# New priorities for the planner of an attention and two-layer expert kernel, and one scaling moved from POOL to ScalarE

## The chip, the cores and the metric

The kernel runs on one core of a Trainium2 chip. Times are device microseconds of one execution. A run is repeated and its median is given; a profile is one further execution, which has its own time and its own span (first to last instruction). The engines are TensorE (PE: matmuls, and PEld for its weight loads), VectorE (DVE), ScalarE (ACT), GpSimd (POOL) and SyncE (SP), which issues most transfers.

## The reference

Three stages follow each other on 4 batches x 576 positions x 512 features.

```python
# 1 attention: q, k, v of (4, 8, 576, 64)
q_d, k_d, v_d = means over groups of 4 positions        # 144 of them
out_d = softmax(q_d k_d^T / 8) v_d, each row repeated 4 times
scores = q k^T / 8 where |i - j| < 4, else -1e9
x = out_d + softmax(scores) v                            # then (2304, 512)
# 2 experts: one of 8 for each token
e = argmax(x w_gate);  g = softmax(x w_gate)[e] * sigmoid(x w_output_gate)[e]
x = g * (relu(x w1[e]) w2[e])                            # 512 -> 1024 -> 512
# 3 a dense layer
h = relu(x w_in);  out = (h * h) w_out                   # 512 -> 2048 -> 512
```

## The kernel before, in words

**Attention** goes by batch. For each batch `b` the keys and queries are loaded in two halves (`load`), folded to 144 positions (`fold`: keys on VectorE, queries on POOL) and the keys are copied into block form on ScalarE (`kb`). The coarse attention has five units `u` per batch: scores (`ds_s`, TensorE), maximum (`ds_m`, VectorE), its scaling (`ds_b`, ScalarE), exponential (`ds_e`, ScalarE, tile `pd`), a small constant added (`ds_a`, ScalarE), reciprocal (`ds_r`, VectorE), the product (`ds_n`, POOL), transposes (`ds_t`, TensorE), copies out (`ds_c`, ScalarE). `ds_pv` and `ds_po` finish it with the folded values (`vd_p`, `vd_c`). The local attention has three units `t3` per batch, in the same manner: `lc_s` (64 small matmuls, L621), `lc_m`, `lc_d` (VectorE), `lc_e` (ScalarE, tile `e`), `lc_v` (the sum, VectorE, L639), `lc_a` (ScalarE), `lc_r` (VectorE), `lc_n` (POOL), `lc_t` (VectorE), then `pv_mm` (128 small matmuls, L672) with the value tiles of `load_vw`. `pv_ad` adds both results into `xT` (VectorE).

**Routing** of a batch: logits (`rt_l`, `rt_le`, `rt_sel`, `rt_lc`), one-hot choice (`rt_g1`), positions (`rt_pp`, `rt_pos`, `rt_base`), the gate's factor (`rt_g2`, `rt_ex`, `rt_ez`, `rt_sm` at L754, `rt_g3`), lists of tokens (`rt_ids` with the marks of L823, `rt_tk` on TensorE at L836, `rt_to`). The tokens are transposed (`rt_bt`), scaled by the factor on their way out of PSUM (`rt_xs`) and stored to DRAM (`rt_st`). In the last batch copying out (`rt_xe`) and scaling (`rt_xs`) are two steps, and the five tiles are scaled by different engines.

**Experts.** The expert with most tokens after three batches goes first, with 256 rows (index -1). Then all eight go by rank, with fixed capacities of 368 to 208 rows. For each expert: rows are gathered by a list (`gather`, POOL; the list comes from `fa_i` or `fr_i`), transposed (`turn`), and written as a high and a low part (`x_hi` on ScalarE, L1150; `x_lo` on VectorE, L1155); the weights are loaded in four steps each (`load1`, `load2`) and split in the same way (`w1_hi`, `w1_lo` at L1172, `w2_hi`, `w2_lo` at L1179). Each product is three matmuls, high by high, high by low and low by high: `mm_h` (L1189) and `mm_y` (L1213). `y_out` and `y_st` store the result. The dense layer's weights are converted from 64-bit floats beside the experts (`cl`, `cm`, `cb`, `ch`, `cx`), and the **dense layer** runs in six windows of 384 rows (`mm1` at L1363, `mm2` at L1387).

**The order** of all this is made by class `Plan` before the program is built. Every operation is entered with its engine, a duration in ns, a number `prio`, what it depends on, and the ring of buffers it takes. `order` then goes forward in a model of time: among the operations that are ready it takes the one that can start first, and where several can start at the same moment, the one with the lowest `prio`:

```python
c = (t, d["prio"], o)
if best is None or c < best:
    best = c
```

The instructions of each engine, transfers of SyncE included, are issued in the order of these planned starts, and each engine works its own list in order. The planned times themselves are not in the program: on the chip, an instruction starts when what it waits for is there and the one before it on its engine has been issued. `SHIFT` holds a number for a kind of operation, which is added to `prio`. One unit of `prio` is a third of a batch in attention and one step of an expert's loop of eight in the experts.

Of the kernel before, what the change touches and what calls it, by code (L numbers as in the profile page):

```python
# [12 lines left out]
ALU = mybir.AluOpType  # L13
# [33 lines left out]
def bcast(ap, shape):  # L47
    return ap.to_broadcast(shape)


SHIFT = {"cho": -1.28, "cli": -7.75, "cmi": 5.29, "cmo": -13.66, "cz": -0.76, "ds_c": 3.91, "ds_m": -18.08, "h_lo": 1.7,
         "kb": 0.72, "lc_e": 1.51, "lc_m": -6.57, "lc_v": 28.85, "mm2": 5.8, "mm_h": -2.09, "mm_y": -0.22, "pv_ad": -13.75,
         "rt_l": -0.15, "rt_ot": 2.89, "rt_pos": 5.92, "rt_sm": 5.36, "rt_xs": 13.38, "turn": 0.29, "vd_c": 18.07,
         "w2_lo": -7.1}


class Plan:
# [9 lines left out]
    def op(self, kind, key, eng, dur, prio, fn, deps=(), lat=0, dma=0, take=None, pair=()):  # L67


        o = (kind,) + key  # L70
        prio += SHIFT.get(kind, 0)
        if isinstance(dur, list):
            run = []

            def step(last):
                if not run:
                    run.append(fn(*key))
                next(run[0], None)
                for _ in run[0] if last else ():
                    pass  # L80

            for i, d in enumerate(dur):
                last = i == len(dur) - 1
                oi = o if last else o + ("step", i)
                self.ops[oi] = dict(eng=eng, dur=d, prio=prio, fn=lambda last=last: step(last), lat=lat, dma=dma, pair=i in pair,
                                    deps=list(deps) if i == 0 else [o + ("step", i - 1)], take=take if i == 0 else None)
            self.first[o] = o + ("step", 0) if len(dur) > 1 else o
            return
        self.ops[o] = dict(eng=eng, dur=dur, prio=prio, fn=lambda: fn(*key), deps=list(deps), lat=lat, dma=dma, take=take, pair=0 in pair)
# [69 lines left out]
class Kern:  # L159
# [194 lines left out]
    def plan_b(self, b):  # L354
        op = self.plan.op
        s = 3.0 * b
# [16 lines left out]
        for u in range(NPR + 1):  # L373
            tau = s - 1.1 + 0.42 * u
            w = 1.0 if u < NPR else 0.6
            pd = "pd" if u < NPR else "pl"
            k = (b, u)
            op("ds_s", k, "PE", 540, tau, self.ds_s, [("fold", b, nm, t) for nm in "kq" for t in range(2) if u // 2 >= t] + [("ds_s", b - 1, 4)] + [("ds_pv", b - 1, 1)] * (u > 1), take="pds")
            op("ds_m", k, "DVE", 365 * w, tau + 0.06, self.ds_m, [("ds_s",) + k])
            op("ds_b", k, "ACT", 100, tau + 0.1, self.ds_b, [("ds_m",) + k])  # L380
            op("ds_e", k, "ACT", 620 if u < NPR else 310, tau + 0.16, self.ds_e, [("ds_b",) + k] + [("ds_e", b - 1, i) for i in range(5)], take=pd)
            self.plan.give("pds", ("ds_s",) + k, ("ds_e",) + k)
            op("ds_a", k, "ACT", 100, tau + 0.2, self.ds_a, [("ds_e",) + k])
            op("ds_r", k, "DVE", 65, tau + 0.22, self.ds_r, [("ds_a",) + k])
            op("ds_n", k, "POOL", 575, tau + 0.3, self.ds_n, [("ds_r",) + k], pair=(0,))
            op("ds_t", k, "PE", 490 if u < NPR else 260, tau + 0.44, self.ds_t, [("ds_n",) + k, ("ds_pv", b - 1, 1)], take="ptr")
            self.plan.give(pd, ("ds_e",) + k, ("ds_t",) + k)
            op("ds_c", k + (0,), "ACT", 270, tau + 0.5, self.ds_ca, [("ds_t",) + k])
            op("ds_c", k + (1,), "ACT", 270, tau + 0.5, self.ds_cv, [("ds_t",) + k])
            self.plan.give("ptr", ("ds_t",) + k, ("ds_c",) + k + (0,), ("ds_c",) + k + (1,))  # L390
# [5 lines left out]
        for t3 in range(3):  # L396
# [5 lines left out]
            self.plan.give("psc", ("lc_s",) + i, ("lc_d",) + i)  # L402
            op("lc_e", i, "ACT", 530, k + 0.47, self.lc_e, [("lc_d",) + i])
            op("lc_v", i, "DVE", 590, k + 0.54, self.lc_v, [("lc_e",) + i])
            op("lc_a", i, "ACT", 110, k + 0.54, self.lc_a, [("lc_v",) + i])
            op("lc_r", i, "DVE", 160, k + 0.54, self.lc_r, [("lc_a",) + i])
            op("lc_n", i, "POOL", 970, k - 0.38, self.lc_n, [("lc_r",) + i], pair=(0,))
            op("lc_t", i, "DVE", 610, k + 0.78, self.lc_t, [("lc_n",) + i], take="pT")
# [37 lines left out]
        for t in range(TPB):  # L446
# [4 lines left out]
            if last:  # L451
                op("rt_xe", (b, t), "ACT", 480, tau + 0.38 + 0.08 * t, self.rt_xe, [("rt_bt", b, t)], take=ring)
                self.plan.give("ptr", ("rt_bt", b, t), ("rt_xe", b, t))
                op("rt_xs", (b, t), ("ACT", "ACT", "POOL", "DVE", "ACT")[t], (600, 600, 1230, 400, 600)[t], tau + 0.19, self.rt_xs, [("rt_xe", b, t), ("rt_g3", b)])
            else:
                op("rt_xs", (b, t), "ACT", 580, tau + 0.4 + 0.08 * t, self.rt_xs, [("rt_bt", b, t)], take=ring)
                self.plan.give("ptr", ("rt_bt", b, t), ("rt_xs", b, t))
# [319 lines left out]
    def rt_xs(self, b, t):  # L777
# [4 lines left out]
            nc.scalar.activation(xo[:n], self.T.pop(("bt", b, t))[:n].rearrange("p c d -> p (c d)"), AF.Copy, scale=s[:n, t:t + 1])  # L782
            return
        xo = self.T["xo", b, t]
        if t == 2:
            nc.gpsimd.tensor_tensor(xo[:n], xo[:n], bcast(s[:n, t:t + 1], [n, DM]), op=ALU.mult)
        elif t != 3:
            nc.scalar.activation(xo[:n], xo[:n], AF.Copy, scale=s[:n, t:t + 1])
        else:
            nc.vector.tensor_scalar(xo[:n], xo[:n], s[:n, t:t + 1], None, op0=ALU.mult)  # L790
# [845 lines left out]
```

## Time and profile before

| | |
|---|---|
| median of 3 runs | 820.26 us (lowest 819.17) |
| profiled execution | 819.88 us, span 818.1 us |
| mean granted clock of TensorE | 0.966 |
| TensorE busy | 763.2 us, 93% |
| VectorE busy | 462.5 us, 57% |
| ScalarE busy | 373.2 us, 46% |
| POOL busy | 117.0 us, 14% |

Busy shares are averages over the whole span. Attention and routing take about the first fifth of it, the experts end near 400 us, and the dense layer takes the rest. The granted clock is the share of full speed that TensorE got, 1.00 for 2.4 GHz and 0.50 for 1.2 GHz; over a stretch it is a mean of the two.

### The profile page before, as it was taken

To read this page: it belongs to the slowest core of one execution; us is meant where nothing else is said; L and a number is where in the kernel's file an instruction comes from. 1 tells how busy PE (TensorE), PEld (TensorE's weight loads), DVE (VectorE), ACT (ScalarE), POOL (GpSimd) and SP (SyncE) were. 2 spreads that over 40 slices of the span, in tenths; PEclk is the share of its full clock that TensorE was granted. 3 is DMA by queue.
4 is the path that set the end of the run, shared out by engine and by line. 5 is a ranking of instruction groups with operands and counts; after the bars stand their busy time and mean duration, and the time that the engine had idled before them with its cause. 6 is when DMAs were issued, how large, how long until landed. Compare 5 with 4: busy or idle time off the path is not lost.

```text
span 818.1 us, 16969 instructions
## 1 busy us (share of the span) xinstructions
PE 763.2 (93%) x6764; PEld 688.6 (84%) x6764; DVE 462.5 (57%) x1022; ACT 373.2 (46%) x801; POOL 117.0 (14%) x150
## 2 busy tenths in 40 slices
PE   3788888698999999999999999999999999999994
PEld 2556566698999999999999989988999999999993
DVE  7647464666877788888687774275223223223221
ACT  9864574544565566667454532222223223222221
POOL 7634220120110110000123301010001001001001
PEclk9968998699999999999999999999999999999997
DMA  9534554667676688787343402011002001001001
GB/s 358 205 94 132 170 174 147 204 204 230 217 226 204 219 251 258 236 251 248 128 142 126 141 1 78 1 40 39 1 1 77 1 1 40 1 0 39 1 1 41
DMA packets 65092, 100.77 MB, mean 123 GB/s; under 512 B 4956, under 2 KB 43356, under 8 KB 65008
## 3 DMA queue, kind: packets, MB, share of 16 engines
q1 hardware_dynamic: 61888, 89.68, 33.9%
q0 software_dynamic: 3120, 9.95, 3.5%
q8 instruction: 55, 0.90, 0.5%
q14 instruction: 29, 0.24, 0.1%
HBM read 80.23 MB, written 19.38 MB: 122 GB/s over the span
## 4 chain that ended last, share of the span: by engine, by line
PE 80%; issue 9%; DVE 3%; ACT 1%; DMA 1%; POOL 0%; another core or an unknown queue 0%; POOLq 0%; DVEq 0%; ACTq 0%
PE hp L1363 21%; PE op L1387 20%; PE hp L1189 14%; PE yp L1213 13%; PE po L672 2%; PE sc L621 1%; PE tp L770 1%; PE dsp L600 1%; PE xp L1144 1%; DMA r<-in_moe_w_dram 1%; PE tp L690 1%; PE tp L568 1%; PE tp L701 1%; PE dsp L522 1%; PE tp L569 1%
## 5 line engine op out<-in xcount | busy, mean ns | idle before, releaser
L1363 PE MATMUL hp<-yh,winh 128*128 128x384 f32 x384 | 129.5, 337 | 0.0
L1363 PE MATMUL hp<-yh,winl 128*128 128x384 f32 x384 | 129.4, 337 | 0.0
L1363 PE MATMUL hp<-yl,winh 128*128 128x384 f32 x384 | 129.3, 337 | 0.0
L1371 DVE SCALAR_TENSOR_TENSOR r<-hp,r 128x384 f32<-128x384 f32 x96 | 53.4, 557 | 120.5 <-ACT r L1368 120.1
L1368 ACT ACTIVATE r<-hp 128x384 f32<-128x384 f32 x96 | 47.2, 492 | 153.5 <-PE hp L1363 143.9
L1387 PE MATMUL op<-woh,hl 128*128 128x512 f32 x288 | 113.8, 395 | 0.2 <-DVE hl L1379 0.2
L1387 PE MATMUL op<-woh,hh 128*128 128x512 f32 x288 | 113.8, 395 | 0.0
L1387 PE MATMUL op<-wol,hh 128*128 128x512 f32 x288 | 113.0, 392 | 0.0
L1379 DVE TENSOR_TENSOR hl<-r,hh 128x384 fp32r<-128x384 f32 x96 | 56.7, 592 | 93.0 <-ACT hh L1375 93.0
L1375 ACT ACTIVATE hh<-r 128x384 fp32r<-128x384 f32 x96 | 50.3, 524 | 112.9 <-PE op L1387 112.2
L1189 PE MATMUL hp<-xh,w1h 128*128 128x256 f32 (+7 forms) x288 | 87.2, 303 | 7.0 <-DVE k L826 5.6
L1189 PE MATMUL hp<-xl,w1h 128*128 128x256 f32 (+7 forms) x288 | 86.5, 300 | 1.5 <-DVE xl L1155 1.5
L1189 PE MATMUL hp<-xh,w1l 128*128 128x256 f32 (+7 forms) x288 | 86.4, 300 | 0.0
L1213 PE MATMUL yp<-hh,w2h 128*128 128x368 f32 (+7 forms) x256 | 76.1, 297 | 0.0
L1213 PE MATMUL yp<-hl,w2h 128*128 128x368 f32 (+7 forms) x256 | 75.8, 296 | 0.0
L1213 PE MATMUL yp<-hh,w2l 128*128 128x368 f32 (+7 forms) x256 | 75.8, 296 | 0.0
L1363 PEld LDWEIGHTS hp<-yh,winh 128*128 128x128 f32 x384 | 72.1, 188 | 3.7
L1363 PEld LDWEIGHTS hp<-yl,winh 128*128 128x128 f32 x384 | 72.1, 188 | 3.6
L1363 PEld LDWEIGHTS hp<-yh,winl 128*128 128x128 f32 x384 | 72.1, 188 | 0.0
L1387 PEld LDWEIGHTS op<-woh,hl 128*128 128x128 f32 x288 | 54.0, 188 | 13.4 <-DVE hl L1379 0.6
L1397 POOL DMA_INDIRECT out_dram<-oo,tidc x18 | 17.9, 993 | 316.2 <-DVE oo L1392 191.0
L1189 PEld LDWEIGHTS hp<-xh,w1h 128*128 128x128 f32 x288 | 55.9, 194 | 7.7 <-issue 5.9
(276 smaller groups left out, 1459.7 us busy)
## 6 DMA issues: line engine op xcount, KB each, us to landing
r<-in_moe_w_dram SPq DMA_DIRECT2D x72, 512.0 KB
raw<-in_moe_w_in_dram SPq DMA_DIRECT2D x16, 512.0 KB
raw<-in_moe_w_out_dram SPq DMA_DIRECT2D x16, 512.0 KB
vw<-in_v_dram SPq DMA_DIRECT2D x12, 512.0 KB
kT<-in_k_dram SPq DMA_DIRECT2D x8, 576.0 KB
qT<-in_q_dram SPq DMA_DIRECT2D x8, 576.0 KB
yT_dram<-zero SPq DMA_DIRECT2D x8, 576.0 KB
yr<-yT_dram SPq DMA_DIRECT2D x6, 768.0 KB
```

The lines of the kernel that those rows point to most:

```text
L522: nc.tensor.matmul(out=sv[:, 0, :], lhsT=qdbd[:, u, 0:P], rhs=kds[:, u], start=True, stop=True)
L568: nc.tensor.transpose(out=tq[:, P * a:P * a + P], in_=pf[:, a, 0:P], identity=ident)
L672: nc.tensor.matmul(out=po[HD * a:HD * a + HD, i, c0:c0 + QB], lhsT=vw[r, g2, 2 * pr + a, :], rhs=pT[r, g2 * 8 + pr * 2 + a, 0:QB], start=T ...
L1189: nc.tensor.matmul(out=ps[:, :cap], lhsT=a[:, k, :], rhs=b[:, k, :cap], start=(n == 0), stop=(n == 11))
L1213: nc.tensor.matmul(out=Y[r][c][:, :cap], lhsT=a[:, P * c:P * c + P], rhs=b[:, :cap], start=(f == 0 and n == 0), stop=(f == 7 and n == 2))
L1363: nc.tensor.matmul(out=ps[:, :WN], lhsT=a[:, k, :], rhs=b[:, k, :], start=(n == 0), stop=(n == 11))
L1368: nc.scalar.activation(r, PS[w, f][:, :WN], AF.Relu)
L1371: nc.vector.scalar_tensor_tensor(SQ[w, f], PS[w, f][:, :WN], 0.0, SQ[w, f], op0=ALU.max, op1=ALU.mult)
L1375: nc.scalar.activation(SQ[w, f, 1][0], SQ[w, f], AF.Copy)
L1379: nc.vector.tensor_tensor(sl, SQ[w, f], sh.bitcast(F32), op=ALU.subtract)
L1387: nc.tensor.matmul(out=O[w][t], lhsT=a[:, P * t:P * t + P], rhs=b, start=(f == 0 and n == 0), stop=(f == 15 and n == 2))
L1397: ins = nc.gpsimd.indirect_dma_start(out=self.out, out_offset=bass.IndirectOffsetOnAxis(ap=self.tidc[:, 3 * w + t:3 * w + t + 1], axis=0), ...
```

## The change

`SHIFT` is replaced by a table of other numbers, and it can now also hold a number for one batch, one expert or one setup step of a kind: `"lc_s:3"` is the local scores of batch 3, `"turn:0"` the transposes of the first ranked expert, `"w1_lo:-1"` the low first-layer weights of the early expert, `"cz:sel"` the setup step `sel`. Such a number is added to that of its kind. Two durations that the planner uses are raised, those of `ds_a` and `lc_a`. In the last batch the scaling of tile 2 moves from POOL to ScalarE, in the plan and in the program. Kinds that are no longer in the table (`cmi`, `lc_v` without a batch, `mm_y`, `rt_sm`, `w2_lo` and others) go back to no shift. Nothing else differs: apart from that scaling every instruction is the same.

```diff
--- before.py
+++ after.py
@@ -48,10 +48,14 @@
     return ap.to_broadcast(shape)
 
 
-SHIFT = {"cho": -1.28, "cli": -7.75, "cmi": 5.29, "cmo": -13.66, "cz": -0.76, "ds_c": 3.91, "ds_m": -18.08, "h_lo": 1.7,
-         "kb": 0.72, "lc_e": 1.51, "lc_m": -6.57, "lc_v": 28.85, "mm2": 5.8, "mm_h": -2.09, "mm_y": -0.22, "pv_ad": -13.75,
-         "rt_l": -0.15, "rt_ot": 2.89, "rt_pos": 5.92, "rt_sm": 5.36, "rt_xs": 13.38, "turn": 0.29, "vd_c": 18.07,
-         "w2_lo": -7.1}
+SHIFT = {"cho": -7.05, "cli": -6.63, "cmo": -9.74, "cz:pn2": 0.51, "cz:qd1": -1.14, "cz:sel": 17.29, "cz:tri": 3.98,
+         "ds_a": 2.2, "ds_c": 3.14, "ds_c:0": 0.13, "ds_c:1": -17.69, "ds_e": 2.74, "ds_m": -16.61, "ds_pv:3": 2.23,
+         "ds_r": -2.37, "ds_t:0": -1.38, "ds_t:1": 2.98, "ds_t:3": -0.27, "fr_i:0": 6.28, "h_lo:-1": 1.97, "kb:1": 6.47,
+         "kb:2": -12.83, "lc_e": 4.13, "lc_m": -1.86, "lc_n": -0.86, "lc_n:1": -2.11, "lc_r": -1.14, "lc_r:1": 0.6,
+         "lc_s:2": 4.65, "lc_s:3": 8.3, "lc_v:0": 7.03, "lc_v:1": 6.09, "load_vw:0": -8.32, "mm2": 5.54, "mm_h": -1.92,
+         "pv_ad": -20.14, "pv_mm:1": 3.06, "pv_mm:2": 0.13, "rt_base:0": 4.94, "rt_bt:0": 1.18, "rt_g2": -11.79,
+         "rt_l:2": -0.17, "rt_ot": -4.8, "rt_ot:1": 1.18, "rt_pos": 5.97, "rt_sel:0": 2.2, "rt_tk:1": 3.47, "rt_xs": 12.75,
+         "turn": 0.53, "turn:0": -4.59, "vd_c": 9.22, "vd_p:3": 3.55, "w1_lo:-1": 1.19, "y_out": -4.5}
 
 
 class Plan:
@@ -68,7 +72,7 @@
 
 
         o = (kind,) + key
-        prio += SHIFT.get(kind, 0)
+        prio += SHIFT.get(kind, 0) + SHIFT.get(f"{kind}:{key[0]}" if key else "", 0)
         if isinstance(dur, list):
             run = []
 
@@ -380,7 +384,7 @@
             op("ds_b", k, "ACT", 100, tau + 0.1, self.ds_b, [("ds_m",) + k])
             op("ds_e", k, "ACT", 620 if u < NPR else 310, tau + 0.16, self.ds_e, [("ds_b",) + k] + [("ds_e", b - 1, i) for i in range(5)], take=pd)
             self.plan.give("pds", ("ds_s",) + k, ("ds_e",) + k)
-            op("ds_a", k, "ACT", 100, tau + 0.2, self.ds_a, [("ds_e",) + k])
+            op("ds_a", k, "ACT", 185, tau + 0.2, self.ds_a, [("ds_e",) + k])
             op("ds_r", k, "DVE", 65, tau + 0.22, self.ds_r, [("ds_a",) + k])
             op("ds_n", k, "POOL", 575, tau + 0.3, self.ds_n, [("ds_r",) + k], pair=(0,))
             op("ds_t", k, "PE", 490 if u < NPR else 260, tau + 0.44, self.ds_t, [("ds_n",) + k, ("ds_pv", b - 1, 1)], take="ptr")
@@ -402,7 +406,7 @@
             self.plan.give("psc", ("lc_s",) + i, ("lc_d",) + i)
             op("lc_e", i, "ACT", 530, k + 0.47, self.lc_e, [("lc_d",) + i])
             op("lc_v", i, "DVE", 590, k + 0.54, self.lc_v, [("lc_e",) + i])
-            op("lc_a", i, "ACT", 110, k + 0.54, self.lc_a, [("lc_v",) + i])
+            op("lc_a", i, "ACT", 195, k + 0.54, self.lc_a, [("lc_v",) + i])
             op("lc_r", i, "DVE", 160, k + 0.54, self.lc_r, [("lc_a",) + i])
             op("lc_n", i, "POOL", 970, k - 0.38, self.lc_n, [("lc_r",) + i], pair=(0,))
             op("lc_t", i, "DVE", 610, k + 0.78, self.lc_t, [("lc_n",) + i], take="pT")
@@ -451,7 +455,7 @@
             if last:
                 op("rt_xe", (b, t), "ACT", 480, tau + 0.38 + 0.08 * t, self.rt_xe, [("rt_bt", b, t)], take=ring)
                 self.plan.give("ptr", ("rt_bt", b, t), ("rt_xe", b, t))
-                op("rt_xs", (b, t), ("ACT", "ACT", "POOL", "DVE", "ACT")[t], (600, 600, 1230, 400, 600)[t], tau + 0.19, self.rt_xs, [("rt_xe", b, t), ("rt_g3", b)])
+                op("rt_xs", (b, t), ("ACT", "ACT", "ACT", "DVE", "ACT")[t], (600, 600, 600, 400, 600)[t], tau + 0.19, self.rt_xs, [("rt_xe", b, t), ("rt_g3", b)])
             else:
                 op("rt_xs", (b, t), "ACT", 580, tau + 0.4 + 0.08 * t, self.rt_xs, [("rt_bt", b, t)], take=ring)
                 self.plan.give("ptr", ("rt_bt", b, t), ("rt_xs", b, t))
@@ -782,9 +786,7 @@
             nc.scalar.activation(xo[:n], self.T.pop(("bt", b, t))[:n].rearrange("p c d -> p (c d)"), AF.Copy, scale=s[:n, t:t + 1])
             return
         xo = self.T["xo", b, t]
-        if t == 2:
-            nc.gpsimd.tensor_tensor(xo[:n], xo[:n], bcast(s[:n, t:t + 1], [n, DM]), op=ALU.mult)
-        elif t != 3:
+        if t != 3:
             nc.scalar.activation(xo[:n], xo[:n], AF.Copy, scale=s[:n, t:t + 1])
         else:
             nc.vector.tensor_scalar(xo[:n], xo[:n], s[:n, t:t + 1], None, op0=ALU.mult)
```

## Rows read from the trace of the kernel before

**Rows 1.** Stretches: length; busy PE, PEld, DVE, ACT, POOL; clock, DMA share, GB/s

```profile
0.00:20.00 20.00, 6.69 (x110) 4.72 (x114) 14.80 (x48) 19.00 (x20) 14.07 (x40) 1.00 0.93 357
20.00:135.00 115.00, 96.14 (x2603) 69.12 (x2592) 69.94 (x201) 71.32 (x220) 37.46 (x53) 0.90 0.44 144
135.00:165.00 30.00, 21.86 (x244) 18.03 (x242) 18.45 (x61) 14.61 (x29) 3.15 (x3) 0.66 0.68 221
165.00:200.00 35.00, 31.68 (x226) 30.80 (x225) 19.75 (x42) 15.48 (x31) 7.46 (x7) 0.95 0.73 229
200.00:807.00 607.00, 606.47 (x3602) 565.90 (x3600) 339.11 (x673) 252.22 (x502) 52.06 (x46) 1.00 0.32 101
```

**Rows 2.** TensorE in order of time, two local score runs: start, us, operation

```profile
23.59 1.10 PE L621 MATMUL sc<-kbd,qT 128*32 128x64 f32 x64
...
60.37 1.94 PE L621 MATMUL sc<-kbd,qT 128*32 128x64 f32 x64
```

**Rows 3.** Waits of TensorE, 20 to 135 us: total, times, longest

```profile
PE po L672 <- issue: 6.3, 6, 2.2
PE dsp L526 <- issue: 3.8, 1, 3.8
PE dsp L526 <- ACT pd L544: 1.6, 2, 0.9
PE dsp L522 <- ACT pd L544: 1.5, 1, 1.5
```

**Rows 4.** POOL in order of time, the scaling that moves

```profile
153.44 1.04 POOL L786 TENSOR_TENSOR xo<-xo,s 128x512 f32<-128x512 f32 x1 [7.15 <-DVE pi L818]
```

**Rows 5.** VectorE in order of time, 151 to 157 us

```profile
151.18 0.68 DVE L1179 TENSOR_TENSOR w2l<-r,w2h 128x512 fp32r<-128x512 f32 x1
...
152.15 0.19 DVE L754 TENSOR_REDUCE sm<-ex 128x5 f32<-128x40 f32 x1
...
153.44 1.32 DVE L790 TENSOR_SCALAR xo<-xo,s 128x512 f32<-128x512 f32 x1
154.68 0.81 DVE L823 TENSOR_TENSOR bm<-iob,pi 128x640 bf16<-128x640 f32 x1
155.42 0.68 DVE L1155 TENSOR_TENSOR xl<-hp,xh 128x512 fp32r<-128x512 f32 x1
...
156.73 0.68 DVE L1155 TENSOR_TENSOR xl<-hp,xh 128x512 fp32r<-128x512 f32 x1
```

**Rows 6.** Instructions of line L1311: ns min/median/max, first and last start

```profile
L1311 DVE TENSOR_SCALAR f<-f x32: 411/422/1066, 198.7 to 468.9; 128x512 f32<-128x512 f32 x32
```

**Rows 7.** ScalarE in order of time, 150 to 155 us

```profile
150.66 0.58 ACT L1150 ACTIVATE xh<-hp 128x512 fp32r<-128x512 f32 x1
153.38 1.33 ACT L788 ACTIVATE xo<-xo,s 128x512 f32<-128x512 f32 x2 [2.15 <-DVE pi L818]
154.62 0.57 ACT L1150 ACTIVATE xh<-hp 128x512 fp32r<-128x512 f32 x1
```

**Rows 8.** Waits of TensorE, 135 to 200 us

```profile
PE hp L1189 <- DVE k L826: 5.6, 1, 5.6
PE hp L1189 <- DVE xl L1155: 1.5, 2, 0.8
PE hp L1189 <- ACT xh L1150: 1.5, 1, 1.5
```

**Rows 9.** TensorE in order of time, two instructions between 170 and 187 us

```profile
170.56 0.35 PE L836 MATMUL tp<-dg,bm 128*128 128x80 bf16 x5
...
186.69 0.44 PE L1189 MATMUL hp<-xh,w1h 128*128 128x368 f32 x1 [1.46 <-ACT xh L1150]
```

**Rows 10.** DMA issues, the value tiles: count, size

```profile
vw<-in_v_dram SPq DMA_DIRECT2D x12, 512.0 KB
```

**Rows 11.** Waits of TensorE, 0 to 20 us

```profile
PE dsp L522 <- ACT pd L544: 4.8, 1, 4.8
```

**Rows 12.** Waits of VectorE, 20 to 160 us, the local softmax's sum

```profile
DVE lsm L639 <- ACT e L635: 3.7, 4, 1.1
```

## The prediction

> **What bounds the kernel now.** I began with the busy times by stretch, then read the waits of the stretches with holes, then the instruction order in the two worst holes. From 200 us on TensorE is busy for 606.47 of 607 us at a granted clock of 1.00 [rows 1]. That part has a fixed length, and the end of the kernel is the moment at which it begins plus that length. VectorE and ScalarE have 339 and 252 us of work in these 607, so they cover their own reordering there. Everything that this change can give or take lies before 200 us.
>
> There TensorE is idle for 13.3 us in the first 20, for 18.9 us from 20 to 135 (attention), for 8.1 us from 135 to 165 (the last batch's routing and the early expert) and for 3.3 us from 165 to 200 (the start of the first ranked expert): 43.6 us [rows 1]. It is also slow there. The same 64 score matmuls take 1.10 us at 23.6 us and 1.94 us at 60.4 us [rows 2]: the two levels of its clock, 2.4 and 1.2 GHz. Busy time times the missing clock gives what that costs: 0.10 of 96.1, 0.34 of 21.9 and 0.05 of 31.7 are 9.6, 7.4 and 1.6, together 18.6 us [rows 1]. So 62 us stand against the change as a ceiling that no order reaches, because the first loads and the first folds are part of it.
>
> Not all of the idle time is a matter of order. Of the 18.9 us in attention, 6.3 and 3.8 are "issue" [rows 3]: TensorE waited for nothing that the profile shows, mostly between the small matmuls of one instruction run. A priority cannot remove these 10.1 us. The other 8.8 us are waits for work of other engines, the largest named ones for ScalarE's exponentials (`pd`), 1.6 and 1.5.
>
> **Part 1, the scaling moved from POOL to ScalarE.** Removed: one POOL multiply of 1.04 us [rows 4]. It starts at 153.44 us, the same moment as VectorE's scaling of another tile, which takes 1.32 us [rows 5]. The nearest row without POOL beside it is L1311, also a tensor-by-scalar operation on 128x512 from SBUF to SBUF, with a median of 0.42 us [rows 6]. The scaling stands in front of the marks (L823) and the two low parts of the early expert's rows (L1155), and TensorE starts its long run only behind the second of these [rows 5]. Between a gain of 0 (the scalar is a tile here, a constant there) and 0.9 I take 0.9, the value of the nearest row. The Trainium skill ("Advanced Engine Details and Errata", VectorE Performance Modes) says that VectorE's second SBUF port is shared with GpSimd and that the two block each other; by that rule it is 0.9 us, without it 0. Added: one ScalarE scaling, 0.67 us by the pair that takes 1.33 [rows 7]. ScalarE had idled 2.15 us just before that pair, and behind it stands the second high part (154.62 us). If the third scaling goes ahead of it, that ends at 155.9 instead of 155.2; the low part that needs it would, with VectorE 0.9 us earlier, start at 155.8. So the cover is just used up, and the cost is 0 (0.7 if VectorE gains more than that). POOL's queue issues nothing else until the gathers of the first ranked expert, so POOL's relief is worth nothing. **-0.9**
>
> **Part 2, the two model durations.** 100 to 185 ns and 110 to 195 ns issue no instruction. They only move the planner's ScalarE clock, 32 times 85 ns over the four batches. 0 by themselves; they act through the order, counted below.
>
> **Part 3, the order from 135 to 165 us.** TensorE waits 5.6 us for VectorE in front of the early expert [rows 8]. The first high part of its rows is ready at 151.24 us (150.66 + 0.58 [rows 7]), but its low part runs at 155.42 [rows 5]. In between VectorE does low parts of second-layer weights (L1179, 0.6 us from start to start; two of them stand directly ahead), the ordering of experts, and late (152.15 us) the softmax sum of the routing, which is what the scalings wait for. The change takes the low second-layer weights' head start away (-7.1 to 0), moves the softmax sum forward (+5.36 to 0) and the gate product too (to -11.79). The two weight parts behind the rows: 1.2 us. Of the remaining 5.6 - 0.9 - 1.2 = 3.5 us I take a quarter, 0.9: several things must move together (the scale, then ScalarE's scalings, then the second high part). Ends: 0 and the whole 4.7. What is late next is the second high part on ScalarE. **-2.1**
>
> **Part 4, the first ranked expert.** TensorE waits 1.5 us for its high part and 1.5 us for low parts [rows 8]; at 186.69 us one matmul has started and the run waits [rows 9]. Its transposes get a much lower number (-4.06 on balance), but its list of rows gets a higher one (+6.28), and the placing matmul (L836, 170.56 us [rows 9]) behind which that list stands stays where it was. If two list operations fall behind two low weight parts, the gathers and all behind them come 2 x 0.69 = 1.4 us later. Ends: -3.0 and +1.4; I take the middle. **-0.8**
>
> **Part 5, attention, 20 to 135 us.** Some forty numbers change here: the local softmax's sum loses its 28.85 in the last two batches, the additions into `xT` go further ahead, the third batch's key copies go first, the second's later. These are the same instructions on the same engines, and ScalarE and VectorE are busy 71 and 70 of 115 us [rows 1], so neither is the bound; the waits come from order and latency. Ends: all 8.8 us of waits gone, or 4 us more; a quarter gone is my estimate, as in part 3, where I could name the pieces and the named ones came to about a third. **-2.2**
>
> **Part 6, the start.** The first batch's value tiles are asked for before the second batch's keys and queries. Each is 512 KB [rows 10], 1.5 us at the 357 GB/s of that stretch, where the DMA share is 0.93 [rows 1]. Three of them delay the second batch's data by 4.4 us. ScalarE is busy for 19.0 of the first 20 us, and its 4.8 us of delay to TensorE [rows 11] is work, not order. Ends: -4.8 and +4.4; 0 is taken, since ScalarE has the same work to get through in either order.
>
> **Part 7, the clock.** Of the 18.6 us lost, 7.4 hang on the hole that part 3 narrows and 9.6 on attention's. I let a quarter come back, as much as of the waits. **-4.6** (ends 0 and 18.6.) The Trainium skill ("TensorE: Matmul & The Clock Gate", Part 1) puts the warm-up at under 1% of a typical kernel's span and advises against fitting a model to it, since where the change of level falls differs from run to run. By it at most 8.2 us could be had, and none counted on; in this trace the loss is 2.3% of the span.
>
> **The dense part** (second-layer numbers, output copies, conversion of weights): 0. Its cover is the idle 268 us of VectorE and 355 of ScalarE; where it fails, TensorE's idle time is paid in full.
>
> **Sum:** 0.9 + 2.1 + 0.8 + 2.2 + 4.6 = 10.6 us. The profiled execution took 819.88 us (span 818.1), 0.4 under the median of 820.26. 819.9 - 10.6 = 809.3, and 809.7 against the median: 810.
>
> **Rivals.**
> *Larger gain, 0.25.* The order fits the chip better than a quarter: part 1, all of part 3 (4.7), half of the rest (1.5, 4.4 and 9.3): 20.8 us, 799. For it: the holes are latencies, not work. Against: 10.1 us of issue time and the busy start stay.
> *No change, 0.13.* Each wait removed returns as another, because the planner picks among ready operations by earliest start and the number only breaks ties; many new numbers then give nearly the old order. For it: waits in attention are short and spread over many causes. 819.5.
> *The clock does not follow, 0.10.* Waits shrink as forecast, but the slow stretches stay where they are: 6.0 us, 814. This is the skill's advice above, carried out.
> *Slower, 0.10.* VectorE blocks on the local softmax's sum. Its number falls while that of the exponential before it rises (1.51 to 4.13). VectorE takes its instructions in order, so where ScalarE is later than planned, the maxima, additions and transposes behind the sum wait, and then TensorE. Before, 4 of 12 sums waited, 3.7 us in all, 1.1 at most [rows 12]. It decides when the other 8 wait too: 8 x 1.1 = 8.8 us, of which some two thirds reach TensorE: 826; if the clock falls in those holes, about as much again.
>
> **How the numbers follow.** Forecast 0.42. The range 797 to 823 leaves out the best part of the larger gain (0.07) and most of the slower case (0.08). 2% is 16.4 us, about what a measurement of this kernel can tell from no change. Below 803.9: the larger gain almost whole and the lower edge of the forecast, 0.27. Above 836.7: half of the slower case, 0.05. The rest, 0.68, lies within.
>
> **What would show it.** VectorE's scaling at about 0.42 us; TensorE's 5.6 us wait at 3 or less; the dense part starting some 10 us earlier and as long as before; a clock above 0.90 and 0.66 in the two stretches; the issue time near 10 us. I am wrong if the dense part shows holes, if the clock alone moves the sum, or if VectorE's waits for the exponential grow.

## The result, and the profile after

The kernel after took a median of 809.54 us (805.0 to 811.17, 12 runs) against 818.35 us for the kernel before on the same chip (12 runs): a ratio of 0.9897, 95% interval 0.9871 to 0.9924, so 8.8 us or 1.0% less by the medians. One of the 12 runs of before took 2564.57 us; the ratio leaves it out, and without it the medians are 8.0 us apart. Its profiled execution took 811.17 us with a span of 809.3 us, 8.8 us less than the 818.1 us of before.

To see where they come from I mark four events that every kernel has: the selection matmul of the last batch (**sel**, L701 before, L705 after), the second matmul of the early expert's run (**run**), the last second-layer group of the experts (**last y**), and the end. From the last y to the end both kernels take 413.4 us.

| us | to sel | sel to run | run to last y | span |
|---|---|---|---|---|
| before | 143.3 | 14.1 | 247.3 | 818.1 |
| after | 145.8 | 8.0 | 242.2 | 809.3 |
| difference | +2.5 | -6.1 | -5.1 | -8.8 |

The work on either side of sel is not quite the same. Of the last batch's 20 transposes (`rt_bt`), 12 stand behind sel in the order of before and 4 in that of after; the other 8 go ahead of it. Four of them take 0.66 us at the higher clock and 1.12 at the lower (143.21 us in after), so 1.3 to 2.2 of the +2.5 us are theirs. In the kernel before they cost nothing behind sel, since TensorE then waits anyway. First a row of before, then two of after:

```profile
145.81 2.91 PE L770 MATMUL tp<-ident,xT 128*128 128x128 f32 x12 [0.33 <-DVE lg L705]
```

```profile
145.27 0.66 PE L774 MATMUL tp<-ident,xT 128*128 128x128 f32 x4
...
146.92 0.60 PE L774 MATMUL tp<-ident,xT 128*64 128x128 f32 x4
```

Busy time by stretch of the kernel after, with the columns of [rows 1], which it answers:

```profile
0.00:20.00 20.00, 7.59 (x138) 5.39 (x138) 13.80 (x39) 18.25 (x18) 13.48 (x39) 0.89 0.93 358
20.00:135.00 115.00, 98.80 (x2566) 72.01 (x2567) 74.56 (x215) 72.02 (x222) 38.24 (x53) 0.84 0.47 151
135.00:165.00 30.00, 21.86 (x267) 18.22 (x267) 20.01 (x69) 16.11 (x32) 3.80 (x4) 0.77 0.64 212
165.00:200.00 35.00, 35.00 (x255) 34.91 (x254) 25.73 (x46) 19.99 (x39) 10.38 (x9) 1.00 0.86 279
```

From 165 to 200 us TensorE now has no hole (31.68 us busy before) and the full clock. In attention the clock is lower in this profile than in that of before (0.84 against 0.90), and the clock's loss, reckoned as in the prediction, rose from 18.6 to 21.6 us (0.8, 15.8 and 5.0 in the first three stretches). TensorE's waits, 20 to 135 us and then 135 to 200 us, answering [rows 3, 8]:

```profile
PE po L676 <- issue: 5.7, 4, 2.7
PE tp L774 <- issue: 2.9, 1, 2.9
PE sc L618 <- DVE e L634: 1.2, 1, 1.2
...
PE po L676 <- issue: 3.4, 1, 3.4
PE tp L734 <- DVE oh L728: 2.5, 1, 2.5
PE hp L1191 <- DVE xo L792: 1.8, 1, 1.8
```

The 5.6 us in front of the early expert are 1.8 now, but 2.5 for the one-hot choice are new, and the waits of the first ranked expert (1.5 and 1.5) are gone. The rows of 5.6 and 1.8 name the instruction that VectorE had ended last (`k`, `xo`), which the matmul does not read. What it needs is the first low part of the rows, which sets its buffer free, and the second high part, which it reads. Before, the first low part ended last (155.42 and 0.68), and after, the second high part on ScalarE:

```profile
152.43 0.58 ACT L1152 ACTIVATE xh<-hp 128x512 fp32r<-128x512 f32 x1
```

Why the run comes earlier, VectorE's list in order of time shows; first a few rows of before that [rows 5] does not hold, then those of after:

```profile
145.51 0.24 DVE L705 COPY lg<-tp 128x80 f32<-128x80 f32 x1 [2.16 <-PE tp L701]
...
147.66 0.20 DVE L724 SCALAR_TENSOR_TENSOR oh<-m,eq 128x40 bf16<-128x40 f32 x1
...
149.01 0.69 DVE L1172 TENSOR_TENSOR w1l<-r,w1h 128x512 fp32r<-128x512 f32 x1 [0.91 <-ACT w1h L1169]
...
153.24 0.21 DVE L915 TENSOR_REDUCE eri<-er 128x8 int32<-128x64 f32 x1
```

```profile
147.11 0.24 DVE L709 COPY lg<-tp 128x80 f32<-128x80 f32 x1 [0.94 <-PE tp L705]
147.27 0.68 DVE L1174 TENSOR_TENSOR w1l<-r,w1h 128x512 fp32r<-128x512 f32 x1
...
149.39 0.69 DVE L1181 TENSOR_TENSOR w2l<-r,w2h 128x512 fp32r<-128x512 f32 x1
...
150.22 0.20 DVE L728 SCALAR_TENSOR_TENSOR oh<-m,eq 128x40 bf16<-128x40 f32 x1
...
151.78 0.68 DVE L1157 TENSOR_TENSOR xl<-hp,xh 128x512 fp32r<-128x512 f32 x1
152.56 0.48 DVE L792 TENSOR_SCALAR xo<-xo,s 128x512 f32<-128x512 f32 x1
153.04 0.69 DVE L1157 TENSOR_TENSOR xl<-hp,xh 128x512 fp32r<-128x512 f32 x1
...
154.50 0.82 DVE L825 TENSOR_TENSOR bm<-iob,pi 128x640 bf16<-128x640 f32 x1
```

The list runs from the copy of the last logits (`lg`) to the second low part of the rows (`xl`), behind which TensorE's run starts. Before it takes 11.2 us (145.51 to 156.73): six weight splits, eight steps of ranking the experts (L894 to L920, the last but one is shown), marks and scaling. After it takes 5.9 us (147.11 to 153.04): four splits, one ranking step, the scaling at 0.48 us, and the marks stand behind the rows. The other half is on TensorE and POOL: the placing matmul, and the gathers of the early and of the first ranked expert.

```profile
145.78 1.29 PE L705 MATMUL tp<-sel,L 128*128 128x16 f32 x10
...
153.79 0.58 PE L1191 MATMUL hp<-xl,w1h 128*128 128x256 f32 x1
...
158.85 0.35 PE L838 MATMUL tp<-dg,bm 128*128 128x80 bf16 x5
```

```profile
141.06 1.16 POOL L1139 DMA_INDIRECT xg<-xs_dram,idxa  x1 [17.48 <-DMA r<-in_moe_w_dram]
...
163.00 1.39 POOL L1139 DMA_INDIRECT xg<-xs_dram,idx  x1 [19.52 <-DVE tg L956]
```

The same gathers in the kernel before:

```profile
143.87 1.16 POOL L1137 DMA_INDIRECT xg<-xs_dram,idxa  x1 [21.26 <-DMA r<-in_moe_w_dram]
...
174.09 1.18 POOL L1137 DMA_INDIRECT xg<-xs_dram,idx  x1 [19.62 <-DVE idx L957]
```

The placing matmul comes at 158.85 us instead of 170.56 [rows 9], after two groups of the early expert instead of eight, and the ranked expert's gathers go out 11.1 us earlier.

### The profile page after: what moved, and what is told of

Same layout as the page of the kernel before. It is cut to its first block, busy times and chain, and to the rows that moved or that the text cites. A ratio compares the mean times of both kernels' runs of the same rounds, so it can differ in the third digit from the quotient of the medians.

```text
span 809.3 us, 16960 instructions
## 1 busy us (share of the span) xinstructions
PE 761.3 (94%) x6764; PEld 687.7 (85%) x6764; DVE 465.2 (57%) x1022; ACT 373.5 (46%) x802; POOL 117.1 (14%) x149
## 4 chain that ended last, share of the span: by engine, by line
PE 82%; issue 9%; DVE 3%; ACT 2%; POOL 0%; another core or an unknown queue 0%; POOLq 0%; DVEq 0%; ACTq 0%
PE hp L1365 22%; PE op L1389 20%; PE hp L1191 14%; PE yp L1215 14%; PE po L676 2%; PE dsp L604 1%; PE sc L625 1%; PE xp L1146 1%; PE tp L774 1%; PE tp L507 1%; PE tp L694 1%; PE tp L572 1%; PE dsp L526 1%; PE tp L705 1%; PE tp L573 0%
## 5 line engine op out<-in xcount | busy, mean ns | idle before, releaser
L1370 ACT ACTIVATE r<-hp 128x384 f32<-128x384 f32 x96 | 47.2, 492 | 154.2 <-PE hp L1365 143.9
L1389 PEld LDWEIGHTS op<-wol,hh 128*128 128x128 f32 x288 | 54.1, 188 | 9.0
```

The costliest lines, as they stand in the source:

```text
L1370: nc.scalar.activation(r, PS[w, f][:, :WN], AF.Relu)
L1389: nc.tensor.matmul(out=O[w][t], lhsT=a[:, P * t:P * t + P], rhs=b, start=(f == 0 and n == 0), stop=(f == 15 and n == 2))
```

## Experiments

Each kernel was timed against the kernel before on its own chip. Segments are of single profiles.

| kernel | to sel | sel to run | run to last y | ratio to before, 95% |
|---|---|---|---|---|
| rows_first | 146.3 | 12.4 | 246.9 | 0.9981 (0.9954 to 1.0008) |
| lists_first | 141.6 | 12.8 | 241.3 | 0.9954 (0.9929 to 0.9978) |
| front_numbers | 142.2 | 8.2 | 241.9 | 0.9891 (0.9852 to 0.9929) |
| undo_both | 141.2 | 11.2 | 246.1 | 0.9951 (0.9929 to 0.9974) |
| rows_free | 148.0 | 14.1 | 244.7 | 1.0004 (0.9976 to 1.0032) |
| rows_free_first | 147.6 | 10.7 | 249.1 | 1.0007 (0.9982 to 1.0032) |
| scale_alone | 140.9 | 13.3 | 248.4 | 1.0003 (0.9980 to 1.0026) |
| onehot_first | 148.3 | 8.3 | 243.3 | 0.9906 (0.9882 to 0.9929) |
| late_two | 143.5 | 11.9 | 241.6 | 0.9913 (0.9870 to 0.9956) |
| placing_late | 143.9 | 7.9 | 245.7 | 0.9920 (0.9882 to 0.9958) |

**rows_first**: the kernel before, low parts forced ahead of marks and scalings, placing matmul held back.

```diff
-    self.rt_ids, [("rt_pos", b), ("rt_tk", b - 1), ("rt_ot", b)]
+    self.rt_ids, [..., ("x_lo", -1, 1)]          # last batch
-    self.rt_tk, [("rt_ids", b)]
+    self.rt_tk, [("rt_ids", b), ("mm_h", -1, 7)] # last batch
-    self.rt_xs, [("rt_xe", b, t), ("rt_g3", b)]
+    self.rt_xs, [..., ("x_hi", -1, 1)]           # last batch
```

> The kernel before, with one thing forced: in the last batch the scalings and the marks are ordered behind the early expert's high and low parts; the placing matmul of the lists is held behind the early expert's first eight groups, where it was. Theory A (the gain lies behind attention, in two orders): TensorE's 5.6 us wait before the early expert falls to 2 or less, the expert's run begins some 5 us earlier after the last batch's selection matmuls (14.1 us before, 8.0 in the changed kernel), attention unchanged, and the total falls by 5 to 6 us. Theory B (the forecast's shares: attention and clock 4.6, this stretch 4.9 through the second-layer weights' and the softmax sum's numbers and the scaling): these numbers are not touched and POOL still scales, so the total falls by 2 us or less.

Measured 817.89 us against 818.62. The stretch sel to run fell by 1.7 us in the profile, the total by nothing that can be told. Putting the rows first is not the gain by itself, and theory A does not hold: six splits and 13 ranking steps still stood in VectorE's list (9.5 us), and TensorE waited 2.4 us for gathered rows.

**lists_first**: the kernel before with one number more.

```diff
-         "w2_lo": -7.1}
+         "w2_lo": -7.1, "rt_tk:3": -3}
```

> The kernel before, with one number added: the last batch's placing matmul of the lists gets -3, so that it stands behind the early expert's first group instead of its eighth. Theory A: the gathers of the first ranked expert go out some 10 us earlier, TensorE's waits of 3 us between 165 and 200 us go, and the total falls by 4 to 5 us. Theory B (this stage was priced at 0.8 us, 3.0 at most): 1 to 3 us.

815.09 us. The placing matmul runs at 156.91 us, and run to last y falls from 247.3 to 241.3 in the profile. By the runs, alone this is worth 0.46% (0.22 to 0.71%), 1.8 to 5.8 us, which does not decide between the two theories.

**front_numbers**: the table of after for attention, setup and the routing of batches 0 to 2, and its two durations; the old numbers for the last batch's routing, the experts and the dense layer; the scaling on POOL.

```diff
-         "turn": 0.53, "turn:0": -4.59, ... "w1_lo:-1": 1.19, "y_out": -4.5}
+         "turn": 0.29, ... "w2_lo": -7.1, "rt_sm:3": 5.36, "rt_xs:3": 13.38, "mm_y": -0.22}
+        if t == 2:
+            nc.gpsimd.tensor_tensor(xo[:n], xo[:n], bcast(s[:n, t:t + 1], [n, DM]), op=ALU.mult)
```

> The changed table for attention, setup and the routing of the first three batches with the two new durations; the table of before for the last batch's routing, the experts and the dense layer, and the scaling on POOL. Its TensorE order is the changed kernel's. Theory A (what moved the order behind attention is the planned end of attention, not the numbers of that stretch): as fast as the changed kernel within 2 us, about 811, VectorE's scaling at 1.3 us again. Theory B: the 3.9 us of the stretch's own numbers and of the scaling, and the 1.2 of the ranked expert's are missing, 814 to 815.

809.17 us, the same as the kernel after, and TensorE's instructions come in the order of after throughout. So the numbers for early work made the late order, and the numbers for late work and the moved scaling are worth nothing that its six runs can tell (some 3 us to either side). VectorE's list in it:

```profile
148.12 0.69 DVE L1159 TENSOR_TENSOR xl<-hp,xh 128x512 fp32r<-128x512 f32 x1
148.72 0.55 DVE L898 SCALAR_TENSOR_TENSOR nr<-ra,base 128x8 f32<-128x8 f32 x1
...
149.30 0.47 DVE L794 TENSOR_SCALAR xo<-xo,s 128x512 f32<-128x512 f32 x1
149.70 0.68 DVE L1159 TENSOR_TENSOR xl<-hp,xh 128x512 fp32r<-128x512 f32 x1
```

and POOL's scaling, which ended just before VectorE's began:

```profile
148.21 1.04 POOL L790 TENSOR_TENSOR xo<-xo,s 128x512 f32<-128x512 f32 x1 [7.69 <-DVE base L816]
```

**undo_both**: the kernel after with both late orders put back.

```diff
-    self.rt_tk, [("rt_ids", b)]
+    self.rt_tk, [("rt_ids", b), ("mm_h", -1, 7)]            # last batch
-    x_lo, [("x_hi", r, k)]
+    x_lo, [("x_hi", r, k), ("rt_ids", NB - 1) ...]          # early expert
-    x_hi, [("turn", r, k)]
+    x_hi, [("turn", r, k), ("rt_xs", NB - 1, 1)]            # early expert, k = 1
```

> The changed kernel with the two orders behind attention forced back: the early expert's low parts behind the marks and its second high part behind the second scaling, and the placing matmul behind the expert's eighth group. Attention is the changed kernel's. Theory A: all of the gain goes, and what is left is attention, 2.5 us longer in the trace: 818 to 822. Theory B: attention and the clock keep their 4.6 us and ScalarE's scaling 0.9: 812 to 814.

815.26 us, ratio 0.9951 where that of after is 0.9897: undoing both loses about half of the gain, so theory A does not hold as it stands. The 0.49% that stayed (0.26 to 0.71%, 2.1 to 5.8 us) do not hang on the two late orders. Four splits instead of six in the list (8.3 us) account for part of it; the rest may be attention or the clock, which is not settled (see part 7).

By now I held that the gain needs two things at once: gathered rows that come early, and the order. The next two test that.

**rows_free** and **rows_free_first**: the early expert's gather reads the input `v`, so it waits for no store (the early expert then computes on other data); alone, and with the edits of rows_first.

```diff
-    in_=self.xs[0:S * (NB - 1), :] if r < 0 else self.xs
+    in_=<v as rows of 512>[0:S * (NB - 1), :] if r < 0 else self.xs
```

> Kernel before with one thing changed: the early expert's gather reads rows of the input v instead of the stored tokens, so it need not wait for the last store of the third batch (the early expert then computes on other data). Every engine keeps its order of before. In the kernel before that gather went out at 143.87 us, 6.5 us after the last store was issued (137.32), and the stretch from the last batch's selection matmul to the early expert's run took 14.1 us. Theory C (the rows must come early AND the planner must put them ahead of the scalings and marks; neither is worth anything alone): the gather goes out some 4 us earlier, the low parts of the rows still stand behind scaling and marks on VectorE, the stretch stays at 13 to 14 us: 817 to 819, ratio 0.998 to 1.001. Rival R (early rows alone are the gain): stretch about 9 to 10 us, 813 to 815, ratio 0.993 to 0.996.

> rows_first (order of before, but the early expert's low parts ahead of scalings and marks, placing matmul held after the eight groups; it gave a ratio of 0.9981) with the gather freed from the stores as in rows_free. Theory C: now the order has something to work on: the stretch from selection to the early expert's run falls from 12.4 us in rows_first to 8 or 9, 3 to 5 us below rows_first: about 813, ratio 0.992 to 0.995. Rival R: like rows_free. Rival O (neither matters, the stretch is set by the chain of the one-hot choice on VectorE): like rows_first, 817, ratio 0.997 to 1.000.

Neither gained. In rows_free the gather goes out at 139.85 us, 12.5 us ahead of the one-hot choice (152.31), and TensorE waits as long as before. The row names a step of the marks; what the matmul needs is the low part that VectorE ended just ahead of it:

```profile
PE hp L1193 <- DVE k L830: 5.6, 1, 5.6
```

In rows_free_first it waits for VectorE again, for the first low part, and the row names the ranking step behind it:

```profile
PE hp L1193 <- DVE offe L927: 4.3, 1, 4.3
...
PE hp L1193 <- DVE xl L1159: 1.1, 1, 1.1
```

My joint theory fell: early rows and the rows' order together give a stretch of 10.7 us, not 8 or 9, and no shorter total. What stays is VectorE's list itself, with its splits and ranking steps (8.7 us here).

**scale_alone**: the kernel before, only the scaling moved.

```diff
-        if t == 2:
-            nc.gpsimd.tensor_tensor(xo[:n], xo[:n], bcast(s[:n, t:t + 1], [n, DM]), op=ALU.mult)
-        elif t != 3:
+        if t != 3:
```

> Kernel before with the third scaling issued on ScalarE instead of POOL, every other instruction in the order of before. The recorded step says -0.9 us: VectorE's scaling falls from 1.32 to about 0.45 us and stands ahead of the marks and of the low parts that TensorE waits for. Theory P1 (the recorded step): 817.6, ratio 0.9985 to 0.9995, VectorE's scaling at 0.48. Rival N (ScalarE's one more scaling, 0.67 us, delays the second high part, so that the gain is lost there): VectorE's scaling at 0.48, and ratio 0.9995 to 1.0005.

VectorE in order of time:

```profile
151.07 0.48 DVE L792 TENSOR_SCALAR xo<-xo,s 128x512 f32<-128x512 f32 x1
151.47 0.82 DVE L825 TENSOR_TENSOR bm<-iob,pi 128x640 bf16<-128x640 f32 x1
152.20 0.68 DVE L1157 TENSOR_TENSOR xl<-hp,xh 128x512 fp32r<-128x512 f32 x1
153.51 0.68 DVE L1157 TENSOR_TENSOR xl<-hp,xh 128x512 fp32r<-128x512 f32 x1
```

1.32 became 0.48 us, the list fell from 11.2 to 10.4 and sel to run from 14.1 to 13.3. The total does not show it: 0.8 us is 0.1%, and the interval is 0.2% to either side. The two theories differ by less than that; the segment speaks for the recorded step. ScalarE's cover is used up, as the recorded step reckoned: its second high part ends at 153.44 us, and the low part that needs it starts at 153.51.

**onehot_first**: the kernel after, four splits held behind the one-hot choice.

```diff
-    w1_lo, [("w1_hi", r, f)]
+    w1_lo, [("w1_hi", r, f), ("rt_g1", NB - 1)]   # early expert, f = 2, 3; w2_lo likewise
```

> Kernel after, with four of the early expert's low weight parts (steps 2 and 3 of both layers) held until the last batch's one-hot choice is made. In the kernel after they stand between the steps of that choice on VectorE (0.6 us each from start to start, 147.27 to 149.99) and TensorE waits 2.5 us for the one-hot. Theory W (a wait of TensorE in front of its long run is worth what it is): one-hot 2.4 us earlier, all of it kept: ratio to before about 0.9868, 807.5. Theory V (VectorE is busy without a gap from the logits to the low parts of the rows, so the same four parts are only moved behind the choice and still lie ahead of the rows): the wait of 2.5 goes to under 0.5, the early expert's run starts at most 0.7 us earlier after the selection matmul: ratio 0.988 to 0.990, not to be told from the kernel after.

810.86 us, ratio 0.9906: as the kernel after. TensorE's waits in it, 138 to 165 us:

```profile
PE hp L1191 <- DVE xl L1157: 2.0, 1, 2.0
PE hp L1191 <- DVE hal L1205: 1.2, 1, 1.2
PE tp L734 <- DVE oh L728: 0.6, 1, 0.6
```

The wait for the one-hot fell from 2.5 to 0.6 us. The wait in front of the run went from 1.8 to 2.0, now for the low part, and 1.2 in the first groups are new: the same splits were still to be done ahead of the run, and VectorE's list is 5.4 us instead of 5.9. That sel to run is 8.3 us all the same, with 1.7 us less of waits, has to do with the clock of this profile, in which the selection takes 2.15 us instead of 1.29. A wait for an engine that has a full list is not worth its length.

**late_two**: the kernel before, its attention numbers too, with only VectorE's list cleared and the placing matmul moved up: the edits of rows_first without the one for `rt_tk`, and

```diff
-    self.fr_a, [("rt_base", NB - 1)]
+    self.fr_a, [("rt_base", NB - 1), ("x_lo", -1, 1)]
-         "w2_lo": -7.1}
+         "w2_lo": -7.1, "rt_tk:3": -3}
```

> Kernel before, attention numbers and all, with two things done in the late stretch alone: (1) VectorE's list between the last batch's logits and the second low part of the early expert's rows is cleared of the ranking of experts, the marks and the scaling (in the kernel before that list takes 11.2 us: 6 weight splits, 8 ranking steps, marks, scaling, 3.1 us idle; in the kernel after 5.9 us: 4 splits, 1 ranking step); (2) the number of the last batch's placing matmul is lowered by 3, so that it runs between the early expert's groups. Theory V (VectorE's list sets the early expert's run, the placing matmul's place sets the first ranked expert, and nothing else was gained): from selection to run 9 to 10.5 us instead of 14.1, from run to the last second-layer group 241 to 243 instead of 247: ratio 0.988 to 0.991, 809 to 811. Theory A (the attention's new numbers carry 3 to 5 us of the gain): ratio 0.993 to 0.996. Rival D (list_first's 0.9954 is all that such a change can give, since the rows land too late for a shorter list: second gather landing about 150): ratio 0.995.

809.98 us against 818.56, ratio 0.9913: as much as the kernel after, without one of the new numbers, but by six runs, whose interval (3.6 to 10.6 us) takes in most of theory A's range too. (Of the 3.1 us of idle time named in the expectation, 2.2 lie ahead of the logits' copy.) Its waits, its low parts on VectorE, and the placing matmul:

```profile
PE hp L1148 <- DMA xg<-xs_dram,idxa: 3.9, 1, 3.9
PE hp L1193 <- ACT xh L1154: 0.7, 1, 0.7
```

```profile
144.86 0.24 DVE L709 COPY lg<-tp 128x80 f32<-128x80 f32 x1 [1.02 <-PE tp L705]
...
153.69 0.69 DVE L1159 TENSOR_TENSOR xl<-hp,xh 128x512 fp32r<-128x512 f32 x1 [1.78 <-ACT xh L1154]
154.66 0.69 DVE L1159 TENSOR_TENSOR xl<-hp,xh 128x512 fp32r<-128x512 f32 x1 [0.29 <-ACT xh L1154]
```

```profile
161.29 0.35 PE L840 MATMUL tp<-dg,bm 128*128 128x80 bf16 x5
```

With the list cleared, VectorE waits itself, and the gathered rows are what is late (3.9 us): sel to run is 11.9 us, not the 9 to 10.5 expected. That is where early rows would count, and by these rows why the kernel after, with both, has 8.0; no run adds early rows to late_two.

**placing_late**: the kernel after with the `rt_tk` edit of rows_first alone.

> Kernel after with one dependency: the last batch's placing matmul is held until the eighth group of the early expert has been issued, as in the order of before. Theory V: the first ranked expert's lists come 8 to 10 us later, from run to the last second-layer group 247 instead of 242, selection to run unchanged at 8: ratio to before 0.994 to 0.996, 814 to 815. Rival H (the early placing is hidden, because the ranked expert waits for its weights anyway): as the kernel after, 0.989 to 0.991.

811.63 us, ratio 0.9920: between the two theories, and the interval takes in both. The placing matmul comes at 165.19 us and the ranked expert's gather at

```profile
168.72 1.17 POOL L1139 DMA_INDIRECT xg<-xs_dram,idx  x1 [26.47 <-DVE idx L959]
```

that is 5.7 us later than in after, not 8 to 10: the early expert ran early here, so the eight groups were over sooner. The waits of the ranked expert are back, 165 to 200 us:

```profile
PE hp L1191 <- ACT xh L1152: 1.6, 1, 1.6
PE yp L1215 <- DVE tok L846: 0.5, 1, 0.5
PE hp L1191 <- DVE xl L1157: 0.5, 1, 0.5
```

Over all profiles the place of that matmul separates run to last y cleanly: 241.3 to 243.3 us in the five kernels where it is early, 244.7 to 249.1 in the seven where it is late, means 242.1 and 246.9.

**att_before** and **att_after**: both kernels cut off behind the last logits (`held` opens buffers; `late` is twelve operations that are left out of both, so that the work is the same).

```diff
             fns = self.plan.order()
+            cut = fns.index(O["rt_lc", NB - 1]["fn"])
+            fns = [f for i, f in enumerate(fns) if id(f) in held or (i <= cut and id(f) not in late)]
```

> Kernel before cut off behind the copy of the last batch's logits on VectorE (everything planned later is left out: the experts, the dense layer, the rest of the last routing, also the early expert's gathers; no output is written). Only the pair with att_after counts, which does exactly the same work in the order of after. This one should end near 146 us plus what lies around the span, some 148 to 160. The ratio to the whole kernel has no meaning.

> The same cut in the order of after, with the same instructions as att_before. The recorded steps say: attention 2.2 us shorter by waits and about 2.4 us (the half of the clock's 4.6 that hangs on attention) by the clock: 4 to 5 us below att_before. Theory V (all of the gain lies behind the last logits): within 1 us of att_before. The single profiles of the two whole kernels say 2.5 us longer.

150.00 us (145.61 to 152.08, 6 runs) and 147.42 us (145.89 to 147.75, 4 runs). The order of after is 2.6 us shorter by the medians, but the runs overlap, and the fastest of each, 145.61 and 145.89, say 0.3 us longer. The whole kernels can't settle it either: the seven with the attention order of before reach sel after 140.9 to 148.0 us, mean 144.5, the five with that of after 141.2 to 148.3, mean 144.3, and these have the eight transposes more ahead of it (1.3 to 2.2 us). So attention gave between nothing and some 2.5 us; it stays open.

## Why the prediction was right, and which steps were not

The total came out as forecast (8.8 us against 10.6), but the terms did not. I had put 3.8 us on the late stretch (parts 1, 3, 4) and 6.8 on attention and the clock (parts 5, 7). The two profiles give 11.2 for the late segments and 2.5 against it for attention, and late_two gains as much with the old attention. So the sum is right by luck in its parts: one term too small and others that are not shown made up for each other. That 810 was forecast and 809.54 measured is luck too, since the 820.26 that I started from, a median of three runs, lies some 2 us above the later medians.

**Part 1** was right in kind and size in its stretch (1.32 to 0.48 us, 0.8 us off sel to run), and worth nothing beside the numbers: in front_numbers POOL's scaling ended at 149.25 us, VectorE's began at 149.30 and took 0.47 us. The rule of the Trainium skill weighed there ("Advanced Engine Details and Errata", VectorE Performance Modes: the shared port) agrees with these rows: 1.32 us with POOL's multiply beside it, 0.47 or 0.48 without. In front_numbers it was the ranking step at 148.72 us that met POOL's multiply: 0.55 us instead of 0.16. The low part at 148.12 ran beside it and kept its 0.69.

**Part 2** was not tested alone.

**Part 3** found the right place and the right list, but took a quarter of it and named the wrong numbers. The mis-sized term is the quarter taken of the remaining 3.5 us; sel to run fell by 6.1 us. The list lost two splits (1.2 us from start to start), seven ranking steps (0.9), the marks and lists (1.4), 0.8 on the scaling and 0.9 of idle time, 5.2 of the 5.3 by which it shortened. What is late next is the second high part on ScalarE, as forecast. And the shifts that I made responsible (`w2_lo`, `rt_sm`, the last batch's `rt_g2`) keep their old values in front_numbers, which has the whole gain. What acted were the numbers for earlier work: the third batch's last store was issued at 137.32 us before and in the pair that starts at 133.15 after, so the gather is out 4.7 us ahead of sel instead of 0.55 behind it. That the planner then finds the rows ready before marks and ranking is argued from the order, not shown by a run.

**Part 4** failed in one step, that the placing matmul "stays where it was". Its own number did not change, and it moved up 11.7 us; that this comes of what it competes with in the planner is argued, not shown. The term was -0.8; run to last y fell by 5.1, of which some 3.3 are the holes from 165 to 200 us and 1.6 the clock there (1.00 for 0.95). lists_first, which lowers the number of that matmul alone, is worth 1.8 to 5.8 us.

**Part 5** (-2.2) is neither shown nor refuted. TensorE's idle time ahead of sel, which that term is made of, is 31.9 to 36.9 us in the seven profiles with the order of before (mean 34.6) and 32.3 to 34.9 in the five with that of after (mean 34.0). **Part 6** was misread: in both kernels the first value tiles are asked for at 9.12 us, at the same place of SyncE's queue; the 0 stands for another reason than the one given.

**Part 7** (-4.6) is not shown, and not refuted. In the profile of after the clock in attention fell, but that execution had the lowest granted clock over the whole span of the twelve (0.961; mean 0.970) and the longest time. In the 69 executions of before that the experiments were compared with the mean is 0.966. The difference, 0.004 of some 810 us, is about 3 us, idle time at the lower level included, so up to that much may have come back. undo_both, with the attention order of after and both late orders undone, has 0.969 in the mean of its 12. One profile tells nothing here: from 20 to 135 us the clock was 0.84 to 0.92 in the eight profiles with the attention order of before and 0.84 to 0.93 in the six with that of after. The Trainium skill's advice ("TensorE: Matmul & The Clock Gate", Part 1) not to fit a model to the number of slow matmuls, since it varies from run to run, agrees with these rows. Its figure, under 1%, is said of the ramp; the loss over the whole span, which I set beside it, is another quantity: 18.6 of 818.1 us before and 21.6 of 809.3 after, that is 2.3% and 2.7%. Whether the rival in which the clock does not follow was right on that term stays open. VectorE did not block on the local softmax's sum: its waits there for the exponential are 0.8 us, against 3.7 before [rows 12].

Of the signs I had named, VectorE's 0.48 us, the wait of 1.8 for 5.6 and the dense part that starts 8.8 us earlier and is as long came true, and TensorE's issue time from 20 to 135 us stayed near 10 (8.6). In the profile the clock came above 0.66 from 135 to 165 us but not above 0.90 in attention.

## What to carry to other kernels

When a matmul run waits for an engine that works in order, write out that engine's list from the event that opens it to the one that ends the wait, and mark what the run does not need: that sum (here 5 of 11 us), not a share of the wait, is what a new order can give, up to the next thing that is late (here the gathered rows). An operation can move a long way without a change of its own number, so look also for what it shares an engine with. Where one execution differs from the next by more than the term in question, compare segments in several profiles before crediting a stretch or the clock, and count what stands ahead of the mark in each: here eight transposes had crossed it.

## What the runs showed of the hardware

Seven executions of one instruction order reached the last selection matmul between 140.9 and 148.0 us, nearly as wide as the whole effect. For the same 2855 matmuls ahead of it TensorE was busy for 106.4 to 114.1 us, at a granted clock of 0.92 to 0.84. Meanwhile the medians of the kernel before, in four sets of 11 to 29 runs, lie between 818.35 and 818.62.

The third batch's last store, 128 KB, took 6.2 us from issue to landing in rows_first, with weight loads of 512 KB issued just ahead of it, where those of 256 KB took 2.9. Size alone is not the reason: in the kernel after the 256 KB store issued beside it (133.15 us) took 5.3. The early expert's gather starts 1.0 us after it lands in each of the seven profiles of whole kernels that show the landing (140.05 and 141.06 us in after). The groups of DMA issues, 120 to 150 us, with their size in KB and median us to landing:

```profile
xs_dram<-xo SPq DMA_DIRECT2D x4, 256.0 KB, 2.9
xs_dram<-xo SPq DMA_DIRECT2D x1, 128.0 KB, 6.2
```

That it queues behind the loads was not tested.
